# RWKV mixing and a PReLU feed-forward in one kernel: pair 0's v scaling and w^128 on ScalarE, later loads and check, the last sum in two halves

## The chip, the cores and the metric

The kernel runs on one core of a Trainium2 chip. The metric is the device time of one execution in microseconds; the kernel before took 484.07 us (median of three runs). The engines are TensorE (PE, with its weight loads PEld), VectorE (DVE), ScalarE (ACT), GpSimd (POOL) and SyncE (SP), which here only issues DMAs. Each engine works through its own instructions in order and waits on semaphores for the others.

## The reference

A linear recurrence over 768 steps, for 4 batches and 8 heads of 48, and on its output a feed-forward with two weight matrices:

```
state = 0                                     # per batch and head, 48 x 48
for t in range(768):
    cur = outer(u * k[t], v[t])
    y[t] = r[t] @ (state + cur)
    state = w[:, None] * state + outer(k[t], v[t])
x = y as [3072, 384]                          # tokens x (heads * 48)
h = x @ w_in                                  # [3072, 2048]
g = max(h, 0) + alpha * min(h, 0)
out = g @ w_out                               # [3072, 384]
```

## The kernel before

The sequence is cut into six chunks of 128 steps, the heads into four pairs (q = 0 to 3). In a chunk the recurrence becomes products of matrices: with tables of powers of w (`W[q]`, made by `table`) r and k are scaled, their scores are masked and multiplied with v, and a state goes from chunk to chunk. `T[q]` holds the state of a pair. Products of r, u, k give the factors of the diagonal (`diagonal`), one per step, head and batch.

Chunk 0 (`first_chunk`) has no state before it. For each pair: two loads `r`, `k0`, the two products with the table (L447), their product for the factors (L533), the scores on TensorE (L457), the sums that give the factors (L540, into the accumulator `bank`), v times the factors (L464, into `gh`), the mask by VectorE (L477) and by ScalarE with GpSimd (L471, L473), the output (L485, L489), which is split into a high and a low part (L504, L508). `tokens_table` makes `whalf`, the powers of w by token: ScalarE writes scaled rows (L315), TensorE turns them (L322), VectorE copies them (L325); with it the k of chunk 0 are scaled (L431) and the state made (`state`, L521). `w128` holds w^128 (L279). Chunk 1 ("hasty") takes its products from VectorE (L565), transposes k (L303) and writes its diagonal blocks with GpSimd (L594); `burst` does the hand-over from pair to pair (L652, L662).

The feed-forward runs in 96 steps (6 chunks times 16 blocks of 128 hidden units). `m_in` makes a block of h in nine matmuls (L740), ScalarE and VectorE make g and split it into high and low parts (L748 to L753), `m_out` adds it to three accumulators, one for each 128 output columns (k = 0 to 2), in nine matmuls (L774). At the end of a chunk the sums are copied and stored (L801, L803). Weights come as 64-bit numbers and are taken apart by ScalarE and VectorE (`part_of_tile`). `check` tests that the inputs lie in the range that this form needs, and writes a flag; each engine reads it at a set place of the program (L890), and a general loop follows if it is set.

The order of the work is not that of the code: every piece is given an engine, an estimated time, what it reads and writes, and a rank (`add`), and `Plan.in_order` simulates the engines and lets on each the ready piece with the lowest rank go first. `warm` is a matmul on the identity whose result nobody reads; the plan puts such fillers (`fill`) where TensorE would wait before the first `m_out`.

Of the kernel before, what the change touches and what calls it, by code (L numbers as in the profile page):

```python
# [18 lines left out]
L = 128  # L19
C = S // L  # L20
# [47 lines left out]
class Plan:  # L68
# [24 lines left out]
    def in_order(self):  # L93
# [50 lines left out]
        while any(waiting.values()):  # L144
# [34 lines left out]
def rwkv_prelu_kernel(ctx: ExitStack, tc, rk, vkr, wP, uP, u, wall, alpha, w, r_all, k_all, v_all, oT):  # L179
# [93 lines left out]
    def table(m):  # L273
# [5 lines left out]
        add("DVE", 0.1, lambda: nc.vector.tensor_tensor(  # L279
            out=w128()[:, m:m + 1], in0=t()[:, 128:129], in1=t()[:, 128:129], op=ALU.mult), r=[t], w=[(w128, m)],  # L280
            rank=10 * m - 78)

    def negative():
        add("ACT", 0.2, lambda: nc.scalar.activation(minus(), ident2(), AF.Copy, scale=-1.0), r=[ident2], w=[minus],
# [26 lines left out]
    def tokens_table(n, first, at):  # L311
        rows, pt = sb([112, P, L], "g", 3), psum()
        for m in range(P):
            for j in range(n // HI):
                add("ACT", 0.3, lambda m=m, j=j: nc.scalar.activation(  # L315
                    rows()[:, m, HI * j:HI * (j + 1)], W[m]()[:, L - 1:HI - 1:-1], AF.Copy,
                    scale=w128()[:, m:m + 1] if first and j == 0 else W[m]()[:, L:L + 1]),
                    r=[W[m], (w128, m)], w=[(rows, (m, j))], rank=at)
# [5 lines left out]
        add("PE", 0.6, turn, r=[rows, ident], w=[pt], rank=at)  # L324
# [6 lines left out]
    def raw_weights(i, rank, behind=()):  # L331
        t = raws[i] = sb([128, 2 * DM, 2], "wraw", 2, U32)
        for p, cols, by in parts_of(i):
            load((t, p), lambda cols=cols: nc.sync.dma_start(
                t()[:, cols].rearrange("p f a -> p (f a)"), wall[i][:, cols].bitcast(U32)), 768 * by, rank + (p or 0), behind)
        return t

    def parts_of(i):
        return [(p, slice(DM * p, DM * (p + 1)), 0.5) for p in range(2)] if i == 0 else [(None, slice(0, 2 * DM), 1.0)]
# [44 lines left out]
    first_k, first_v = [], []  # L384
# [30 lines left out]
    def inputs(c, q, r, k0, v, k, early):  # L415
        n = 2 * B * D
        moved = [(X[0], (1, 1, 2))] if c == 1 else []
        for j, t in enumerate((r, k0)):
            if c == q == j == 0:
# [7 lines left out]
             early + 0.1 * q + 0.15 if c else -98.85 + 0.1 * q, moved)  # L427
# [9 lines left out]
    def first_chunk(q):  # L437
# [16 lines left out]
        def scores():  # L454
# [5 lines left out]
        add("PE", 1.1, scores, r=[r, k0], w=A, rank=q - 95)  # L460
# [3 lines left out]
        add("DVE", 0.5, lambda: nc.vector.tensor_tensor(  # L464
            out=vc().rearrange("p b (g e) -> p g b e", g=2)[:, :, :, 0:D],
            in0=v().rearrange("p (g b) e -> p g b e", g=2),
            in1=bank()[:, 8 * q:8 * q + 8].rearrange("p (b g) -> p g b", g=2)[:, :, :, None].broadcast_to([128, 2, B, D]),
            op=ALU.mult), r=[(bank, q), v], w=[vc], rank=10 * q - 77)
# [62 lines left out]
    def diagonal(q, r, k0, cu, sums, cols, mine, prod_rank, sum_rank, copy_rank):  # L531
# [11 lines left out]
        add("PE", 0.6, c_sum, r=[prod, uw], w=[mine], rank=sum_rank)  # L543
# [216 lines left out]
    def m_out(n):  # L760
# [10 lines left out]
        def mm(j, ks):  # L771
            a, x = ((wh, gh), (wl, gh), (wh, gl))[j]
            for k in ks:
                nc.tensor.matmul(banks[k](), a[i]()[:, NK + k], x(), start=(begin and j == 0), stop=(end and j == 2))  # L774

        if n == NM - 1:
            for k in range(NK):
                add("PE", 0.7, lambda k=k: [mm(j, (k,)) for j in range(3)], r=[(wh[i], 1), (wl[i], 1), gh, gl], w=[banks[k]],
                    rank=n + MLAG - 0.5)
# [4 lines left out]
        if end:  # L784
            again = c in seen
            seen.add(c)
            for k in range(NK):
# [7 lines left out]
                if again:  # L795
# [3 lines left out]
                        out=o(), in0=t(), in1=o(), op=ALU.add), r=[banks[k]], w=[o], rank=n - 90)  # L799
                else:  # L800
# [7 lines left out]
    def check():  # L808
# [3 lines left out]
        at = 40  # L812
        add("POOL", 0.1, lambda: (ok(), w2(), nc.gpsimd.memset(ok()[:, 0:NF + P], 0.0)), w=[ok], rank=at)
        add("DVE", 0.1, lambda: nc.vector.tensor_scalar(ok()[:, 0:NF], alph(), 1.0, None, op0=ALU.is_le), r=[alph],
            w=[ok], rank=at)
        add("DVE", 0.1, lambda: nc.vector.tensor_tensor(out=w2(), in0=wp(), in1=wp(), op=ALU.mult), r=[wp], w=[w2],
# [42 lines left out]
    jobs.append((40, 7, check))  # L859
# [158 lines left out]
```

## Time and profile before

| what | value |
|---|---|
| median of three runs | 484.07 us (482.76 to 484.35) |
| profiled execution | 483.28 us |
| span of the profile | 481.6 us |
| TensorE busy | 472.8 us, 98% |
| VectorE busy | 312.1 us, 65% |
| ScalarE busy | 244.8 us, 51% |
| GpSimd busy | 97.6 us, 20% |
| granted TensorE clock | 0.999 |

A row of the order in time gives the start, the duration, the engine, the line, the operation, what is written from what is read, and how many instructions are merged in it; in brackets stands the time for which the engine was idle before it, and what ended this. Matmuls are pipelined, so the durations of neighbours overlap.

### The profile page before, as it was taken

What the parts mean: (1) busy time and instruction counts of PE and PEld (TensorE: products, weight loads), DVE (VectorE), ACT (ScalarE), POOL (GpSimd) and SP (SyncE); (2) the same over time, 40 slices, a digit from 0 to 9 for tenths busy, and PEclk for the clock granted to TensorE, in tenths of its full rate; (3) what the DMA queues carried; (4) which work ended last, traced back from release to release, by engine and by line L of the source; (5) the groups of instructions that cost most, each with busy time, mean ns of one, the idle gap of its engine ahead of it and who ended that gap; (6) DMA issues with size and microseconds to landing.
All of it is one profiled execution on the core that took longest, in us unless ns stands there. A gap on an engine that the chain in (4) does not pass through costs nothing. (4 is left out here: it accounts for less than half of the span.)

```text
span 481.6 us, 11276 instructions
## 1 busy us (share of the span) xinstructions
PE 472.8 (98%) x4667; PEld 385.2 (80%) x4667; DVE 312.1 (65%) x519; ACT 244.8 (51%) x554; POOL 97.6 (20%) x119
## 2 busy tenths in 40 slices
PE   8999999999999999999999999999999999999996
PEld 6777777888888888888888888888888878888884
DVE  7999899999787784865755766745634534333331
ACT  3877898766455553553553643544633433433332
POOL 5119890012414021402202301200200000000000
PEclk9999999999999999999999999999999999999999
DMA  7965785632154631531221421200310000100001
GB/s 227 276 231 181 247 248 167 230 125 74 41 174 123 193 116 59 149 91 37 64 78 37 152 86 40 72 26 31 85 37 1 1 1 0 67 0 1 0 1 69
DMA packets 23111, 46.19 MB, mean 96 GB/s; under 512 B 3376, under 2 KB 11184, under 8 KB 23056
## 3 DMA queue, kind: packets, MB, share of 16 engines
q1 hardware_dynamic: 21968, 43.24, 28.4%
q0 software_dynamic: 960, 1.97, 2.0%
q8 instruction: 37, 0.61, 0.5%
q10 hardware_dynamic: 128, 0.23, 0.1%
q14 instruction: 18, 0.15, 0.1%
HBM read 37.17 MB, written 6.29 MB: 90 GB/s over the span
## 5 line engine op out<-in xcount | busy, mean ns | idle before, releaser
L740 PE MATMUL bank<-x,wh 128*128 128x512 f32 x576 | 195.3, 392 | 0.0
L749 DVE SCALAR_TENSOR_TENSOR g<-bank,alph,g 128x512 f32<-128x512 f32 x96 | 71.9, 749 | 104.5 <-ACT g L748 104.2
L740 PEld LDWEIGHTS bank<-x,wh 128*128 128x128 f32 x576 | 108.1, 188 | 23.9 <-issue 0.8
L748 ACT ACTIVATE g<-bank 128x512 f32<-128x512 f32 x96 | 57.2, 596 | 128.2 <-PE bank L740 127.9
L740 PE MATMUL bank<-x,wl 128*128 128x512 f32 x288 | 112.2, 390 | 0.0
L752 ACT ACTIVATE gh<-g 128x512 fp32r<-128x512 f32 x96 | 60.5, 630 | 73.1 <-DVE g L749 73.0
L753 DVE TENSOR_TENSOR gl<-g,gh 128x512 fp32r<-128x512 f32 x96 | 72.0, 750 | 36.7 <-ACT gh L752 35.9
L774 PE MATMUL acc<-gh,wh 128*128 128x512 f32 x288 | 83.2, 396 | 0.0
L774 PE MATMUL acc<-gh,wl 128*128 128x512 f32 x288 | 81.6, 390 | 0.0
L774 PE MATMUL acc<-gl,wh 128*128 128x512 f32 x288 | 81.5, 390 | 0.0
L774 PEld LDWEIGHTS acc<-gh,wl 128*128 128x128 f32 x288 | 53.9, 188 | 11.4
L774 PEld LDWEIGHTS acc<-gl,wh 128*128 128x128 f32 x288 | 53.9, 188 | 11.3
L740 PEld LDWEIGHTS bank<-x,wl 128*128 128x128 f32 x288 | 54.1, 188 | 10.9
L774 PEld LDWEIGHTS acc<-gh,wh 128*128 128x128 f32 x288 | 52.7, 188 | 11.6 <-issue 0.4
L582 POOL TENSOR_TENSOR rr<-rr,kk 128x384 f32<-128x384 f32 x16 | 20.2, 1261 | 164.0 <-DMA kk<-vkr 89.2
L598 ACT ACTIVATE base<-ident,cu 128x64 f32<-128x64 f32 x128 | 32.9, 337 | 1.8 <-DVE cu L588 1.8
L594 POOL TENSOR_SCALAR base<-ident,cu 128x64 f32<-128x64 f32 x32 | 30.7, 983 | 13.7 <-ACT cu L546 13.7
L406 DVE TENSOR_TENSOR x<-bank,x 48x256 fp32r<-48x256 f32 x64 | 27.0, 422 | 1.3
L390 POOL DMA_DIRECT2D x<-x x30 | 15.4, 519 | 60.6 <-ACT o L801 49.4
L568 DVE TENSOR_TENSOR raw<-raw,W 112x512 f32<-112x512 f32 x32 | 23.7, 764 | 2.5 <-DMA raw<-rk 2.5
L405 ACT ACTIVATE x<-bank 48x256 fp32r<-48x256 f32 x64 | 24.2, 378 | 2.1 <-PE bank L662 1.0
L584 POOL TENSOR_TENSOR rr<-rr,utab 128x384 f32<-128x384 f32 x16 | 22.9, 1429 | 1.2
(116 smaller groups left out, 397.6 us busy)
## 6 DMA issues: line engine op xcount, KB each, us to landing
wraw<-wall SPq DMA_DIRECT2D x15, 768.0 KB, 4.6
raw<-rk SPq DMA_DIRECT2D x45, 224.0 KB, 3.7
v<-vkr SPq DMA_DIRECT2D x24, 192.0 KB, 3.6
kk<-vkr SPq DMA_DIRECT2D x20, 192.0 KB, 4.0
rr<-vkr SPq DMA_DIRECT2D x16, 192.0 KB, 2.5
oT<-o SPq DMA_DIRECT2D x12, 256.0 KB, 2.2
x<-x POOLq DMA_DIRECT2D x30, 64.0 KB, 2.6
oT<-g SPq DMA_DIRECT2D x6, 256.0 KB, 3.4
```

The costliest lines, as they stand in the source:

```text
L405: add("ACT", us, lambda: nc.scalar.activation(h(), view(), AF.Copy), r=[src], w=parts(x, 0, ps), rank=rank)
L406: add("DVE", us + 0.1, lambda: nc.vector.tensor_tensor(out=l(), in0=view(), in1=h(), op=ALU.subtract), r=[src] + parts(x, 0, ps), w=parts( ...
L568: add("DVE", 0.72, lambda t=t, tab=tab: nc.vector.tensor_tensor(out=t().rearrange("p b (j t) -> p (b j) t", j=2), in0=t().rearrange("p b ( ...
L584: add("POOL", 1.2, lambda: nc.gpsimd.tensor_tensor(out=rt().rearrange("p (g b) e -> p g b e", g=2), in0=rt().rearrange("p (g b) e -> p g b ...
L594: add("POOL", 1.0, lambda g=g, b=b: nc.gpsimd.tensor_scalar(base()[:, g, b], ident2(), cu()[:, g, b:b + 1], None, op0=ALU.mult), r=[cu, id ...
L598: add("ACT", 0.32, lambda g=g, b=b: nc.scalar.activation(base()[:, g, b], ident2(), AF.Copy, scale=cu()[:, g, b:b + 1]), r=[cu, ident2], w ...
L740: nc.tensor.matmul(hp()[:, :], a[i]()[:, k], X[c]()[:, x, k], start=(k == 0 and j == 0), stop=(k == NK - 1 and j == 2))
L748: add("ACT", 0.6, lambda: nc.scalar.activation(g(), hp()[:, :], AF.Copy), r=[hp], w=[g], rank=n - 100)
L749: add("DVE", 0.75, lambda: nc.vector.scalar_tensor_tensor(out=g(), in0=hp()[:, :], scalar=alph()[:, i:i + 1], in1=g(), op0=ALU.mult, op1=A ...
L752: add("ACT", 0.64, lambda: nc.scalar.activation(gh(), g(), AF.Copy), r=[g], w=[gh], rank=n - 100)
L753: add("DVE", 0.73, lambda: nc.vector.tensor_tensor(out=gl(), in0=g(), in1=gh(), op=ALU.subtract), r=[g, gh], w=[gl], rank=n - 99)
L774: nc.tensor.matmul(banks[k](), a[i]()[:, NK + k], x(), start=(begin and j == 0), stop=(end and j == 2))
```

## The change

Seven things are changed. (1) For pair 0 of chunk 0, v times its factors is done by ScalarE: one instruction copies the factors, eight multiply a 128x48 piece each. (2) w^128 is made by ScalarE, and the rows for whalf of chunk 0 are one instruction per pair instead of two, in another buffer, earlier. (3) v of chunk 0 is loaded later than r and k0 of the next pairs. (4) The check waits for the last weights. (5) The raw weights of blocks 13 to 15 are loaded in halves. (6) Fillers stand behind the sums of pairs 0 and 1, no longer ahead of the scores of pairs 1 to 3; the planner counts small DMAs otherwise. (7) In the last two steps the matmuls go column block by column block, and the last block's sum is made in two halves of 256 tokens, copied by ScalarE and VectorE, stored from SP's and ScalarE's queue.

```diff
-                dma = max(dma, p.end + 1.5) + p.kb / DMA_RATE
-                p.end = dma + 0.3
+                if p.kb < 16:
+                    p.end += 1.7
+                else:
+                    dma = max(dma, p.end + 1.5) + p.kb / DMA_RATE
+                    p.end = dma + 0.3
...
-        add("DVE", 0.1, lambda: nc.vector.tensor_tensor(
-            out=w128()[:, m:m + 1], in0=t()[:, 128:129], in1=t()[:, 128:129], op=ALU.mult), r=[t], w=[(w128, m)],
-            rank=10 * m - 78)
+        add("ACT", 0.2, lambda: nc.scalar.activation(
+            w128()[:, m:m + 1], t()[:, 128:129], AF.Copy, scale=t()[:, 128:129]), r=[t], w=[(w128, m)], rank=-46)
...
-        for p, cols, by in parts_of(i):
+        for p, cols, by in halves if i == 0 or i >= 13 else parts_of(i):
...
-             early + 0.1 * q + 0.15 if c else -98.85 + 0.1 * q, moved)
+             early + 0.1 * q + 0.15 if c else -98.76 + 0.2 * q, moved)
...
+        if q < 1:
+            factors = sb([128, 2, B], "cu", 2)
+            add("ACT", 0.25, lambda: nc.scalar.activation(
+                factors(), bank()[:, 8 * q:8 * q + 8].rearrange("p (b g) -> p g b", g=2), AF.Copy), r=[(bank, q)],
+                w=[factors], rank=q - 93.9)
+            for b in range(B):
+                for g in range(2):
+                    add("ACT", 0.32, lambda b=b, g=g: nc.scalar.activation(
+                        vc()[:, b, HI * g:HI * g + D], v()[:, g * B + b], AF.Copy, scale=factors()[:, g, b:b + 1]),
+                        r=[factors, v], w=[(vc, (b, g))], rank=q - 93.9)
+        else:
...
-        if n == NM - 1:
+        halves = [slice(0, NT // 2), slice(NT // 2, NT)]
+        if n >= NM - 2:
             for k in range(NK):
...
+                        rank=NM + MLAG - 2.5 + (0.1, 0.2, 0.5)[k] + (0.2 + 0.01 * p) * (n == NM - 1))
...
+                elif n == NM - 1 and k == NK - 1:
+                    for p, cols in enumerate(halves):
+                        if p == 0:
+                            add("ACT", 0.38, lambda o=o, t=banks[k], cols=cols: nc.scalar.activation(
+                                o()[:, cols], t()[:, cols], AF.Copy), r=[(banks[k], p)], w=[(o, p)], rank=n - 90)
+                        else:
+                            add("DVE", 0.42, lambda o=o, t=banks[k], cols=cols: nc.vector.tensor_copy(
+                                o()[:, cols], t()[:, cols]), r=[(banks[k], p)], w=[(o, p)], rank=n - 90)
+                        eng, name = ((nc.sync, "SP"), (nc.scalar, "ACT"))[p]
...
-        at = 40
+        at = 24
...
+    for p in first_scores[1:]:
+        fill[p] = 0
```

The order of VectorE from the first table on, before: `W_95` and `W_96` are the tables of pairs 0 and 1, `g` the product for the sums, `gh` the scaled v.

```order
L275 SCALAR_TENSOR_TENSOR W_95<-wp,unit 112x65
L278 RECIPROCAL W_95<-W_95 112x64
L447 TENSOR_TENSOR raw<-raw,W_95 112x512 x2
L533 TENSOR_TENSOR g<-raw 112x512
L275 SCALAR_TENSOR_TENSOR W_96<-wp,unit 112x65
L278 RECIPROCAL W_96<-W_96 112x64
L447 TENSOR_TENSOR raw<-raw,W_96 112x512 x2
L279 TENSOR_TENSOR w_99<-W_95 112x1
L533 TENSOR_TENSOR g<-raw 112x512
L464 TENSOR_TENSOR gh<-v,acc_162 128x2x4x48
L477 COPY_PREDICATED below_135<-strict,bank_142 128x512
```

The same place on VectorE now:

```order
L278 SCALAR_TENSOR_TENSOR W_95<-wp,unit 112x65
L281 RECIPROCAL W_95<-W_95 112x64
L278 SCALAR_TENSOR_TENSOR W_96<-wp,unit 112x65
L450 TENSOR_TENSOR raw<-raw,W_95 112x512
L281 RECIPROCAL W_96<-W_96 112x64
L450 TENSOR_TENSOR raw<-raw,W_95 112x512
L547 TENSOR_TENSOR g<-raw 112x512
L450 TENSOR_TENSOR raw<-raw,W_96 112x512 x2
L547 TENSOR_TENSOR g<-raw 112x512
L491 COPY_PREDICATED below_135<-strict,bank_142 128x512
```

The table of pair 1 has moved ahead of and in between pair 0's products, and w^128 and the scaled v are gone.

VectorE again, from the mask of pair 2 to the products of pair (1,0) now (before, the copy of whalf and the four scalings of kk stood behind L565, the products of raw with `W_95` for chunk 1):

```order
L491 COPY_PREDICATED below_135<-strict,bank_145 128x512
L326 COPY whalf<-bank_142 128x384
L368 SCALAR_TENSOR_TENSOR wx<-wx,low 128x384
L377 SCALAR_TENSOR_TENSOR wx<-wraw,wx 128x384
L491 COPY_PREDICATED gl<-strict,acc_409 128x512
L478 TENSOR_TENSOR gh<-v,acc_162 128x2x4x48
L381 TENSOR_TENSOR wl_118<-wx,wh_102 128x384
L434 TENSOR_TENSOR kk<-kk,whalf 128x384
L368 SCALAR_TENSOR_TENSOR wx<-wx,low 128x384
L434 TENSOR_TENSOR kk<-kk,whalf 128x384 x2
L377 SCALAR_TENSOR_TENSOR wx<-wraw,wx 128x384
L434 TENSOR_TENSOR kk<-kk,whalf 128x384
```

L582, the products for chunk 1, follows two rows below these.

ScalarE behind the rows of `pick`, now; before, `minus` and the two copies of scores followed there at once:

```order
L282 ACTIVATE w_99<-W_95 112x1
L316 ACTIVATE base<-W_95,w_99 112x128
L282 ACTIVATE w_99<-W_96 112x1
L316 ACTIVATE base<-W_96,w_99 112x128
L485 ACTIVATE below_136<-bank_143 128x512
L469 ACTIVATE cu<-acc_162 128x8
L474 ACTIVATE gh<-v,cu 128x48 x8
L485 ACTIVATE gl<-acc_280 128x512
```

Between the copies of pair 0's and pair 1's scores stand the factors and the eight products.

The end of TensorE, before: `acc_4969`, `acc_4971`, `acc_4973` are the sums of k = 0, 1, 2.

```order
L774 MATMUL acc_4969<-gh,wh_117 128x512
L774 MATMUL acc_4969<-gh,wl_133 128x512
L774 MATMUL acc_4969<-gl,wh_117 128x512
L774 MATMUL acc_4971<-gh,wh_117 128x512
L774 MATMUL acc_4971<-gh,wl_133 128x512
L774 MATMUL acc_4971<-gl,wh_117 128x512
L774 MATMUL acc_4973<-gh,wh_117 128x512
L774 MATMUL acc_4973<-gh,wl_133 128x512
L774 MATMUL acc_4973<-gl,wh_117 128x512
```

And now, with `acc_4970` as k = 2:

```order
L791 MATMUL acc_4968<-gh,wh_117 128x512
L791 MATMUL acc_4968<-gh,wl_133 128x512
L791 MATMUL acc_4968<-gl,wh_117 128x512
L791 MATMUL acc_4970<-gh,wh_116 128x512
L791 MATMUL acc_4970<-gh,wl_132 128x512
L791 MATMUL acc_4970<-gl,wh_116 128x512
L791 MATMUL acc_4970<-gh,wh_117 128x256
L791 MATMUL acc_4970<-gh,wl_133 128x256
L791 MATMUL acc_4970<-gl,wh_117 128x256
L791 MATMUL acc_4970<-gh,wh_117 128x256
L791 MATMUL acc_4970<-gh,wl_133 128x256
L791 MATMUL acc_4970<-gl,wh_117 128x256
```

The sums of k = 0 and 1 are complete nine matmuls ahead of the end, and k = 2 comes last in two halves.

## Rows read from the trace of the kernel before

**Rows 1.** Stretches: us, busy PE, PEld, DVE, ACT, POOL, clock, DMA share, GB/s.

```profile
5.00:10.00 5.00, 4.93 (x62) 3.78 (x60) 4.69 (x9) 0.85 (x2) 2.51 (x6) 1.00 0.95 268
25.00:43.00 18.00, 17.50 (x225) 13.72 (x223) 17.76 (x31) 13.77 (x26) 8.82 (x8) 1.00 0.57 183
90.00:470.00 380.00, 380.00 (x3506) 313.99 (x3505) 228.66 (x378) 174.50 (x404) 51.29 (x54) 1.00 0.22 67
```

**Rows 2.** Order in time, VectorE, from the first table to the check.

```profile
4.28 1.35 DVE L447 TENSOR_TENSOR raw<-raw,W 112x512 f32<-112x512 f32 x2
...
6.27 0.29 DVE L275 TENSOR_TENSOR_SCAN W<-wp,unit 112x65 f32<-112x65 f32 x1
...
7.18 0.69 DVE L447 TENSOR_TENSOR raw<-raw,W 112x512 f32<-112x512 f32 x1
8.08 0.69 DVE L447 TENSOR_TENSOR raw<-raw,W 112x512 f32<-112x512 f32 x1 [0.21 <-DMA raw<-rk]
...
9.80 0.54 DVE L464 TENSOR_TENSOR gh<-v,acc 128x384 f32<-128x384 f32 x1
...
22.21 0.17 DVE L814 TENSOR_SCALAR ok<-alph 128x16 f32<-128x16 f32 x1
...
22.76 0.55 DVE L378 TENSOR_TENSOR wl<-wx,wh 128x384 fp32r<-128x384 f32 x1
...
25.77 0.55 DVE L325 COPY whalf<-bank 128x384 f32<-128x384 f32 x1
...
28.24 0.95 DVE L374 SCALAR_TENSOR_TENSOR wx<-wraw,wx 128x768 uint32<-128x768 uint32 x1
...
31.78 0.68 DVE L533 TENSOR_TENSOR g<-raw 112x512 f32<-112x512 f32 x1
```

**Rows 3.** Groups of instructions to 92 us: busy, mean ns, idle before.

```profile
L652 PE MATMUL bank<-raw,T 48*48 48x64 f32 x128 | 3.0, 221 | 1.0 <-ACT x L717 0.7 <-DVE base L681 0.3
...
L279 DVE TENSOR_TENSOR w<-W 112x1 f32<-112x1 f32 x4 | 1.0, 259 | 0.0
...
L322 PE MATMUL bank<-ident,g 112*128 112x112 f32 x4 | 0.5, 258 | 0.0
```

**Rows 4.** Order in time, TensorE, at the start and the fillers.

```profile
6.28 1.16 PE L457 MATMUL bank<-raw 48*128 48x128 f32 x16
7.37 0.63 PE L540 MATMUL acc<-uw,g 112*64 112x2 f32 x16
7.94 0.83 PE L834 MATMUL acc<-ident 128*128 128x256 bf16 x6
...
25.36 0.39 PE L834 MATMUL acc<-ident 128*128 128x256 bf16 x2
25.91 0.60 PE L303 MATMUL bank<-ident,raw 112*128 112x112 f32 x4 [0.16 <-DVE raw L565]
...
30.91 0.82 PE L834 MATMUL acc<-ident 128*128 128x256 bf16 x6
```

**Rows 5.** Order in time, ScalarE, two scaled rows of 112x64.

```profile
17.51 0.37 ACT L315 ACTIVATE g<-W,w 112x64 f32<-112x64 f32 x1
17.75 0.37 ACT L315 ACTIVATE g<-W 112x64 f32<-112x64 f32 x1
```

**Rows 6.** The tail: order in time, the last store's landing, its stretch.

```profile
476.23 0.39 PE L774 MATMUL acc<-gh,wl 128*128 128x512 f32 x1
...
476.45 0.39 PE L774 MATMUL acc<-gl,wh 128*128 128x512 f32 x1
476.94 0.60 ACT L801 ACTIVATE g<-acc 128x512 f32<-128x512 f32 x1
477.56 0.33 SPq L803 DMA_DIRECT2D oT<-g  x1
...
oT<-g SPq DMA_DIRECT2D x1, 256.0 KB, 2.2
...
477.00:479.00 2.00, 0.00 (x0) 0.00 (x0) 0.00 (x0) 0.54 (x1) 0.00 (x0) 1.00 0.99 375
```

More of the change, by code (lines that the diff above doesn't have):

```diff
@@ L311, in tokens_table @@
     def tokens_table(n, first, at):
-        rows, pt = sb([112, P, L], "g", 3), psum()
+        rows, pt = sb([112, P, L], "base" if first else "g", 3), psum()
         for m in range(P):
[L314 to L318, printed above, removed]
+            add("ACT", 0.3 + 0.1 * first, lambda m=m: nc.scalar.activation(
+                rows()[:, m, 0:n], W[m]()[:, L - 1::-1] if first else W[m]()[:, L - 1:HI - 1:-1], AF.Copy,
+                scale=w128()[:, m:m + 1] if first else W[m]()[:, L:L + 1]),
+                r=[W[m], (w128, m)], w=[(rows, m)], rank=at)
         def turn():
@@ L336, in raw_weights @@
         return t
+    halves = [(p, slice(DM * p, DM * (p + 1)), 0.5) for p in range(2)]
     def parts_of(i):
-        return [(p, slice(DM * p, DM * (p + 1)), 0.5) for p in range(2)] if i == 0 else [(None, slice(0, 2 * DM), 1.0)]
+        return halves if i == 0 else [(None, slice(0, 2 * DM), 1.0)]
     def weights(i, need):
@@ L541, in c_sum @@
                                      stop=True, skip_group_check=True)
-        add("PE", 0.6, c_sum, r=[prod, uw], w=[mine], rank=sum_rank)
+            if cu is None:
+                for _ in range((3, 2, 0, 0)[q]):
+                    warm()
+        add("PE", 0.6 + (0.13 * (3, 2, 0, 0)[q] if cu is None else 0), c_sum, r=[prod, uw], w=[mine], rank=sum_rank)
         if cu is None:
@@ L769, in m_out, with mm @@
         acc_of.append(acc[2])
-        def mm(j, ks):
+        def mm(j, ks, cols=slice(0, NT)):
             a, x = ((wh, gh), (wl, gh), (wh, gl))[j]
             for k in ks:
-                nc.tensor.matmul(banks[k](), a[i]()[:, NK + k], x(), start=(begin and j == 0), stop=(end and j == 2))
-        if n == NM - 1:
+                nc.tensor.matmul(banks[k]()[:, cols], a[i]()[:, NK + k], x()[:, cols], start=(begin and j == 0),
+                                 stop=(end and j == 2), skip_group_check=c == C - 1 and k == NK - 1)
+        halves = [slice(0, NT // 2), slice(NT // 2, NT)]
+        if n >= NM - 2:
             for k in range(NK):
-                add("PE", 0.7, lambda k=k: [mm(j, (k,)) for j in range(3)], r=[(wh[i], 1), (wl[i], 1), gh, gl], w=[banks[k]],
-                    rank=n + MLAG - 0.5)
+                for p, cols in enumerate(halves if n == NM - 1 and k == NK - 1 else [slice(0, NT)]):
+                    add("PE", 0.7 if n < NM - 1 or k < NK - 1 else 0.35,
+                        lambda k=k, cols=cols: [mm(j, (k,), cols) for j in range(3)],
+                        r=[(wh[i], 1), (wl[i], 1), gh, gl], w=[banks[k] if n < NM - 1 or k < NK - 1 else (banks[k], p)],
+                        rank=NM + MLAG - 2.5 + (0.1, 0.2, 0.5)[k] + (0.2 + 0.01 * p) * (n == NM - 1))
         else:
```

28 lines of the change are left out of this document (16 added, 12 removed).

## The prediction

> **What bounds the kernel now.** I read the busy time by stretch first [rows 1]. From 90 to 470 us TensorE is busy 380.00 of 380.00 us: the matmuls of the second half of the kernel stand one behind the other, their number does not change, and no edit in that stretch can shorten the time. Time can come only from before, where TensorE waits or runs fillers, and from the tail behind the last matmul. In the first 43 us the full engine is VectorE: 4.69 of 5 us at 5 to 10, 17.76 of 18 at 25 to 43, while ScalarE has 0.85 of 5 at 5 to 10.
>
> The second view is the order in time on VectorE [rows 2]. The reader is to see a chain without holes: tables, products, the scaling of v, weight pieces, with one wait of 0.21 us at 8.08 for a load. Third, TensorE in order of time [rows 4]: its own waits look small because fillers were put where the planner expected a hole. Six fillers stand at 7.94 (0.83 us), two at 25.36 with a wait behind them until the transposes at 25.91 (0.55), six at 30.91 (0.82). Further on, the hand-over matmuls of L652 (four bursts in chunk 1) wait 1.0 us [rows 3]. So TensorE loses 3.2 us that a quicker VectorE could give back. Last the tail [rows 6]: the last matmul starts at 476.45 and takes 0.39, ScalarE copies for 0.60 from 476.94, the store is issued at 477.56 and lands 2.2 us later, at 479.76; the span ends 1.84 us after that.
>
> The profiled execution took 483.28 us, 1.68 outside its span of 481.6; the median of the three runs is 484.07 (482.76 to 484.35). The sum is made against 483.28, and the gain is then taken from the median.
>
> **The change part by part.**
>
> *What VectorE loses.* The four w^128 instructions go, 1.0 us together [rows 3]; one product of v and its factors goes, 0.54; the first four instructions of the check go from here, 0.55 from 22.21 to the next at 22.76; and the wait of 0.21 goes, because pair 1's two loads now stand ahead of v's in SP's queue [rows 2]. That is 2.30. Neighbours on this engine overlap a little (the pair at 4.28 lasts 1.35 for two), for which I take off 0.3: 2.0 us. Nothing new stands on VectorE, so the product that starts at 31.78 should start at about 29.8. The last three of the check leave too, later.
>
> *What VectorE does in another order.* Table 1 (scan and reciprocal, 0.91 us from 6.27 to 7.18) now stands between pair 0's products, which end at 4.28 + 1.35 + 0.91 = 6.54 and not at 5.63. TensorE's scores began at 6.28, behind the fillers, so they begin 0.3 us later. The copy of whalf and the four k scalings (25.77 to 28.24, 2.47 us) now stand ahead of pair (1,0)'s products, which were ready at 25.77: 25.77 - 2.0 + 2.47 = 26.2. The transposes that wait for them (25.91 before) start at 26.3. In exchange two of the four state products, and whalf's transposes, are already done on TensorE by then, and the fillers at 25.36 and 30.91 are gone.
>
> *What TensorE can give back.* Of 0.83 + 0.55 + 0.82 = 2.2 us of fillers, 0.3 is lost at the first scores: 1.9. Both counts, 2.0 by VectorE and 1.9 by TensorE, meet near the same size; I take the smaller. Bounds: nothing, if a new wait stands where a filler stood, and 1.9 + 1.0 = 2.9 if the waits of L652 go as well.
>
> *What ScalarE takes.* Eight instructions of 128x48 with a scale per partition. The nearest rows are those of 112x64 with such a scale: 0.37 us each, 0.24 from start to start (17.51 to 17.75) [rows 5]. That makes 8 x 0.24 = 1.9 us, at most 8 x 0.37 = 3.0 and, since a shorter tile can be quicker, perhaps 1.6. They begin when the factors are there: scores from 6.58, sums 1.09 later as now (6.28 to 7.37), 0.63 for the sums [rows 4], so 8.3, and with the copy of the factors about 8.5. They end at 10.4 (10.1 to 11.5). ScalarE's hole there covers it: 4.15 of 5 us are free at 5 to 10 [rows 1]. In the worst case pair 0's output on TensorE comes a microsecond later than with 10.4, which the wait until 26.3 behind it takes up. w^128 and the table rows are short and fall into the same hole; ScalarE's evacuations of pair 1 queue behind the eight, and VectorE is not behind those.
>
> The Trainium skill, "ScalarE: Activation LUTs", section "Rules for kernel authors", says to use VectorE and not ScalarE for copies and multiplications. By that rule this part loses: one instruction of 0.54 us becomes eight of 1.9. The trace decides for the edit as long as the hole stands, since it is the full engine that gets lighter.
>
> *Loads and flag.* Bytes stay the same; three weight loads become six, each a further issue of 0.33 us (the issue at 477.56 [rows 6]), for weights that TensorE needs in a stretch without a wait. SP now reads the flag later in its queue, ahead of loads for chunk 3, and would hold these back if the check were late; the check's input is done long before. Both at nothing; without that cover 3 x 0.33 = 1.0 us.
>
> *The tail.* Columns k = 0 and 1 are finished two groups earlier, so their stores are out of the way. At present all three stores run together: the DMA engines are 0.99 busy from 477 to 479 [rows 6]. The last half is copied by VectorE (half of ScalarE's 0.60, with a fixed part: 0.3 to 0.5, I take 0.42), and its store carries 128 KB: 2.2 us less half of what 256 KB take at 375 GB/s (0.34), so 1.86, or up to 2.2 if the fixed part is all of it; I take 2.0. It lands 0.1 + 0.42 + 0.02 + 2.0 = 2.54 us after the last matmul, now 479.76 - 476.84 = 2.92: 0.38 gained. Against it stand six matmuls of 256 columns for three of 512. No row shows one. At half the time each they cost nothing, at the full 0.22 (476.23 to 476.45) 0.66. The nearest rows are four transposes of 112 columns with a full weight load in 0.55 us [rows 3], about 0.10 from start to start, so a weight load does not hold a matmul above 0.11: I take 0.03. Tail: 0.35 gained, between -0.3 and +0.6.
>
> The Trainium skill's start page, "Trainium Kernel Development and Optimization", section "Key Constraints", says that stores from SP's and ScalarE's queues run on the same 16 DMA engines and that a second queue only saves issue time. The share of 0.99 fits it. By the rule the second queue is worth one issue of 0.33 us at most, and less if the first half's issue is already over; my 0.38 counts nothing for parallel transfers.
>
> Sum: 1.9 + 0.35 = 2.25 us; 483.28 becomes 481.0, and the median 484.07 becomes 481.8.
>
> **The rivals.**
> - *The gain is given back in chunk 1.* TensorE arrives 1.9 us earlier at the bursts of L652, whose bases GpSimd writes and whose states pass through ScalarE, and waits there. For it: those are the only real waits now [rows 3]. Against it: the first link of that chain comes earlier too, as it hangs on the product at 31.78. With 1.5 us given back 0.75 is left: 483.3.
> - *More than forecast.* The waits of 1.0 in L652 vanish with the lead of VectorE: 2.25 + 1.0, 480.8. The second half of the check leaving VectorE speaks for it.
> - *Slower.* ScalarE's queue is served in order, and the new order puts weight pieces, which wait for VectorE, ahead of the copies of y out of PSUM that TensorE's next step needs. The wait of 0.7 us on ScalarE in L652 [rows 3] is of this kind. If each of the four bursts waits 1.0 more, that is 4.0 - 2.25 = 1.75 lost: 485.8. It decides once each wait grows by more than 2.25/4 = 0.56. ScalarE's light load in the beginning speaks against it.
> - *The change doesn't do what it says.* TensorE's clock is granted at 1.00, the 2.4 GHz level, in each stretch [rows 1], with fillers right ahead of pair 0's and pair 1's scores; some of these are gone or moved. If the clock were at 1.2 GHz for the scores and sums up to 10 us, some 2 us of work, they would take 2 us more and the gain at the start were gone: only the tail is left, 483.7.
>
> The Trainium skill, "TensorE: Matmul & The Clock Gate", section "Why this matters for your kernels", warns that idle gaps between bursts of matmuls send the clock back to half rate. By that rule the place to look at is the hole ahead of 26.3, about 1 us by my count, where fillers stood; no row of before shows a fall during the work, so it gives no price.
>
> **How the numbers follow.** Forecast 481.8 with a chance of 0.52; more 0.13; given back 0.22; clock 0.04; slower 0.09. Its own range is 480.5 to 483. The range for 8 in 10 runs from 479.8, both bounds of the gains together (2.9 + 0.6 = 3.5) and the spread of the runs, to 484.2, which takes in the rival of the given-back gain. A difference of 0.3%, 1.45 us, is about what a measurement of this kernel can tell from no change: below 482.6 is faster. Nearly all of the first two cases lie there, 0.65 together; the two next are no change, 0.26; slower 0.09.
>
> **What would show it.** In the changed profile: VectorE's product for the sums of pair (1,0) starts near 29.8; the eight ScalarE instructions start near 8.5 and end before 11, before the output of pair 0 on TensorE; TensorE's first transposes of chunk 1 start near 26.3, without fillers ahead; the last matmul near 475 and the last store's landing 2.5 us behind it. The forecast is wrong if L652 waits more than 2 us in all, if the scores of pair 0 start later than 7, if the halved matmuls stand more than 0.15 us apart, or if the granted clock is under 1.00 anywhere between 6 and 470 us.

## The result, and the profile of the changed kernel

The changed kernel is slower by about half a per cent, where the prediction said faster. With two more runs the median of the kernel before is 483.21 us, no longer 484.07. A ratio, here and below, is worked out from all runs of both kernels and is not the quotient of the two medians.

| | before | changed |
|---|---|---|
| median, runs | 483.21 us, 5 (482.75 to 484.35) | 485.65 us, 5 (485.26 to 486.38) |
| ratio | | 1.0055 [1.0042, 1.0067] |
| profiled execution, its span | 483.28, 481.56 | 486.38, 484.66 |
| TensorE idle, 90 to 470 us | 0.00 us | 2.16 us |
| last matmul's end to the span's end | 4.72 us | 5.62 us |

The spans differ by 3.1 us: 2.2 have been lost when the last matmul ends (479.04 against 476.84), 0.9 come behind it. The profiled execution of the changed kernel is the slowest of its five, so the account below covers 3.1 us, while the medians differ by 2.4. The stretches of [rows 1] now read as follows, with the one added in which all the idle time lies:

```profile
5.00:10.00 5.00, 4.01 (x68) 3.17 (x66) 4.56 (x7) 3.02 (x12) 2.92 (x7) 1.00 1.03 270
25.00:43.00 18.00, 17.97 (x220) 13.80 (x220) 16.80 (x27) 14.28 (x28) 9.31 (x12) 1.00 0.66 220
90.00:470.00 380.00, 377.84 (x3494) 311.64 (x3493) 227.40 (x382) 173.36 (x402) 49.69 (x54) 1.00 0.22 66
...
129.00:134.00 5.00, 2.84 (x130) 2.37 (x130) 3.03 (x5) 2.59 (x6) 1.83 (x2) 1.00 0.29 88
```

**The start gained, but half of the forecast.** ScalarE's eight instructions take 1.91 us from 8.44, as forecast. VectorE's product of pair (1,0) starts at 30.62, 1.16 earlier than in [rows 2], where 2.0 were forecast. TensorE gets a new wait of 1.37 us, for a copy of x by ScalarE. In order of time on the three engines:

```profile
8.44 1.91 ACT L474 ACTIVATE gh<-v,cu 128x48 f32<-128x48 f32 x8
...
22.14 0.51 PE L522 MATMUL bank<-x,less 128*128 128x512 f32 x1 [1.37 <-ACT x L518]
...
30.62 0.68 DVE L547 TENSOR_TENSOR g<-raw 112x512 f32<-112x512 f32 x1
```

TensorE reaches the first burst of chunk 2 (the matmuls of L669, L652 before) at 129.10 instead of 130.04: 0.94 us gained, where 1.9 were forecast.

**At 129 us this is lost, three times over.** VectorE in order of time, changed kernel:

```profile
124.90 0.55 DVE L605 TENSOR_REDUCE cu<-rr 128x8 f32<-128x384 f32 x1
125.37 0.74 DVE L766 SCALAR_TENSOR_TENSOR g<-bank,alph,g 128x512 f32<-128x512 f32 x1
126.81 0.69 DVE L770 TENSOR_TENSOR gl<-g,gh 128x512 fp32r<-128x512 f32 x1 [0.70 <-ACT gh L769]
129.49 0.56 DVE L434 TENSOR_TENSOR kk<-kk,whalf 128x384 f32<-128x384 f32 x1 [1.99 <-POOL rr L599]
129.97 0.75 DVE L766 SCALAR_TENSOR_TENSOR g<-bank,alph,g 128x512 f32<-128x512 f32 x1
```

and the same place in the kernel before, with TensorE's burst and ScalarE's small copy L675 (L692 now):

```profile
127.80 0.74 DVE L749 SCALAR_TENSOR_TENSOR g<-bank,alph,g 128x512 f32<-128x512 f32 x1
129.42 0.56 DVE L431 TENSOR_TENSOR kk<-kk,whalf 128x384 f32<-128x384 f32 x1 [0.87 <-POOL rr L582]
...
130.04 0.67 PE L652 MATMUL bank<-raw,T 48*48 48x64 f32 x32
131.03 0.14 ACT L675 ACTIVATE seen_y<-bank 1x2 f32<-1x2 f32 x1
```

The planner has put two instructions in the other order. The scaling of k of pair (3, 0) overwrites what GpSimd's product over rr still reads, so it waits; the product with the slopes of step 19 (L766, L749 before) waits for nothing, but now stands behind it. It reads a PSUM bank that TensorE's burst wants. ScalarE's work on step 19 comes 2.2 us late as well, and with it the small copy L692 for which the rest of the burst waits. TensorE and ScalarE, in order of time:

```profile
129.10 0.32 PE L669 MATMUL bank<-raw,T 48*48 48x64 f32 x4
130.77 0.59 PE L669 MATMUL bank<-raw,T 48*48 48x64 f32 x26 [1.35 <-DVE g L766]
...
133.19 0.14 ACT L692 ACTIVATE seen_y<-bank 1x2 f32<-1x2 f32 x1
133.39 0.32 PE L679 MATMUL bank<-base,v 64*48 64x64 f32 x7 [0.81 <-ACT seen_y L692]
```

From this burst to the next it is 17.13 us now (129.10 to 146.23) and was 14.44 (130.04 to 144.48): 2.69 lost.

**A small one at 152 us.** The check's two matmuls, at 24.9 us in the kernel before, now stand in the full stretch:

```profile
152.19 0.39 PE L757 MATMUL bank<-x,wh 128*128 128x512 f32 x1
152.51 0.21 PE L858 MATMUL bank<-ok,one 128*1 128x20 f32 x2
152.65 0.96 PE L791 MATMUL acc<-gh,wh 128*128 128x512 f32 x3
153.45 0.40 PE L791 MATMUL acc<-gh,wl 128*128 128x512 f32 x1
```

From 152.19 to 153.45 there are 1.26 us for four large matmuls that take 4 x 0.227 elsewhere: 0.35 more. From the next burst to the one behind it (146.23 to 163.07, before 144.48 to 160.96) it is 16.84 us instead of 16.48.

**The tail** [rows 6], last matmuls, copies, stores, and the stores' landing:

```profile
478.76 0.28 PE L791 MATMUL acc<-gl,wh 128*128 128x256 f32 x1
479.14 0.38 ACT L825 ACTIVATE g<-acc 128x256 f32<-128x256 f32 x1 [0.85 <-PEq L931]
479.55 0.33 SPq L831 DMA_DIRECT2D oT<-g  x1
479.56 0.42 DVE L828 COPY g<-acc 128x256 f32<-128x256 f32 x1 [3.79 <-ACT g L825]
480.01 0.39 ACTq L831 DMA_DIRECT2D oT<-g  x1
...
oT<-g SPq DMA_DIRECT2D x1, 128.0 KB, 1.7
oT<-g ACTq DMA_DIRECT2D x1, 128.0 KB, 2.6
```

The halves don't run side by side. ScalarE's copy of the first half starts 0.10 after the last matmul of the second, VectorE's copy 0.04 after ScalarE's has ended, so the last store is issued 0.97 behind the last matmul (0.72 before), and it lands after 2.6 us, with half the bytes. The three other profiles with halves (e1, e2, e6) have the copy at 0.10 and the issue at 0.97, too.

The landing is late in one part only. Sixteen updates of a semaphore tell that a store has landed: fifteen stand 1.85 us behind the issue, the last one 0.74 later (0.08 later in the kernel before). The DMA records show where the late share was: its packets begin at 481.76, where a fetch of 8 KB of instructions ends that had begun at 481.00, and the others are through by 481.4. In the kernel before such a fetch begins at 479.06, when the last packets of the store are already running. In e1, e2, e3 and e6 the late share, too, begins within 0.02 us of the end of such a fetch. That the fetch holds it up is read from these records; no run tests it.

Account: -0.94 at the start, +2.69 at the burst, +0.36 for the check's matmuls, +0.90 for the tail (0.60 up to the last landing, 0.29 behind it), together +3.0 of 3.1.

### The profile page after: what moved, and what is told of

Same layout as the page of the kernel before. It is cut to its first block, busy times and chain, and to the rows that moved or that the text cites. A ratio compares the mean times of both kernels' runs of the same rounds, so it can differ in the third digit from the quotient of the medians.

```text
span 484.7 us, 11264 instructions
## 1 busy us (share of the span) xinstructions
PE 471.9 (97%) x4659; PEld 384.1 (79%) x4659; DVE 311.3 (64%) x515; ACT 247.8 (51%) x563; POOL 91.2 (19%) x119
## 5 line engine op out<-in xcount | busy, mean ns | idle before, releaser
L766 DVE SCALAR_TENSOR_TENSOR g<-bank,alph,g 128x512 f32<-128x512 f32 x96 | 71.9, 749 | 105.0 <-ACT g L765 103.4
L791 PE MATMUL acc<-gh,wh 128*128 128x512 f32 x289 | 84.2, 397 | 0.0
L599 POOL TENSOR_TENSOR rr<-rr,kk 128x384 f32<-128x384 f32 x16 | 18.5, 1156 | 168.1 <-DMA kk<-vkr 91.8
L611 POOL TENSOR_SCALAR base<-ident,cu 128x64 f32<-128x64 f32 x32 | 26.5, 850 | 17.3 <-ACT cu L563 17.3
L585 DVE TENSOR_TENSOR raw<-raw,W 112x512 f32<-112x512 f32 x32 | 22.3, 724 | 3.1 <-DMA raw<-rk 3.1
L601 POOL TENSOR_TENSOR rr<-rr,utab 128x384 f32<-128x384 f32 x16 | 21.7, 1356 | 1.2
```

The lines of the kernel that those rows point to most:

```text
L585: add("DVE", 0.72, lambda t=t, tab=tab: nc.vector.tensor_tensor(out=t().rearrange("p b (j t) -> p (b j) t", j=2), in0=t().rearrange("p b ( ...
L601: add("POOL", 1.2, lambda: nc.gpsimd.tensor_tensor(out=rt().rearrange("p (g b) e -> p g b e", g=2), in0=rt().rearrange("p (g b) e -> p g b ...
L611: add("POOL", 1.0, lambda g=g, b=b: nc.gpsimd.tensor_scalar(base()[:, g, b], ident2(), cu()[:, g, b:b + 1], None, op0=ALU.mult), r=[cu, id ...
L766: add("DVE", 0.75, lambda: nc.vector.scalar_tensor_tensor(out=g(), in0=hp()[:, :], scalar=alph()[:, i:i + 1], in1=g(), op0=ALU.mult, op1=A ...
L791: nc.tensor.matmul(banks[k]()[:, cols], a[i]()[:, NK + k], x()[:, cols], start=(begin and j == 0), stop=(end and j == 2), skip_group_check ...
```

## Experiments

Ratios are to the kernel before on the same chip; 0.001 is 0.48 us. The intervals are 0.8 to 1.7 us wide, so a difference of a few tenths between two runs is read from the profiles, if at all. "Piece" is what the planner orders.

| run | median us | before us | ratio, 95% interval |
|---|---|---|---|
| e1_swap | 483.95 | 483.04 | 1.0012 [1.0002, 1.0022] |
| e2_check_behind | 486.48 | 483.04 | 1.0072 [1.0056, 1.0088] |
| e3_tail_whole | 485.34 | 483.04 | 1.0051 [1.0033, 1.0069] |
| e4_before_swap | 484.99 | 483.04 | 1.0037 [1.0023, 1.0052] |
| e5_swap_tail | 483.06 | 483.32 | 0.9997 [0.9989, 1.0006] |
| e6_order_only | 485.91 | 483.32 | 1.0051 [1.0036, 1.0067] |
| e7_copies_first | 483.23 | 483.32 | 0.9998 [0.9985, 1.0011] |
| e8_v_vector | 483.10 | 483.32 | 1.0000 [0.9985, 1.0014] |
| e9_v_vector | 482.50 | 482.67 | 0.9999 [0.9987, 1.0011] |
| e10_before_v | 482.90 | 482.67 | 1.0001 [0.9990, 1.0012] |
| e11_weights_whole | 482.24 | 482.67 | 0.9986 [0.9977, 0.9995] |
| e12_best | 482.60 | 482.88 | 0.9987 [0.9975, 0.9998] |

### The order on VectorE: e1 and e4

After planning, one piece is moved (e4: the scaling ahead of the product, in the kernel before).

```diff
     order = plan.in_order()
+    order.remove(leaky[19])                              # product of step 19
+    order.insert(order.index(scaled[4]), leaky[19])      # scaling of k, pair (3, 0)
```

> The changed kernel with one exchange on VectorE: the product with the slopes of step 19 stands ahead of the scaling of k of pair (3, 0), which stood ahead of it; nothing else moves. Theory 1 (order): in the changed kernel that scaling waits 1.99 us for GpSimd, the product of step 19 starts at 129.97 for that reason, and TensorE, whose burst wants the PSUM bank that the product reads, stands 1.35 us, and 0.81 us again when ScalarE, pushed back by the same product, frees the other bank late. Then both waits go, step 19's product starts near 128 and the time falls by 2.0 to 2.6, to 483.0 to 483.6. Theory 2 (supply): the burst waits for the scaled k itself, whatever the order, since rr of that pair lands at 128.4; then a wait of 0.8 to 1.3 stands at L643 (L646 in this kernel) in place of the first one, the second goes, and the time is 484.3 to 484.9. Theory 3 (the loss is not in this burst but spread over 90 to 470 us): 485.4 to 485.9.

> The kernel before, with the opposite exchange: the scaling of k of pair (3, 0) ahead of the product with the slopes of step 19, at 127.8 us; nothing else moves. Theory 1 (order): the product starts near 130.0 instead of 127.80, the burst that began at 130.04 waits 0.6 to 0.8 for its bank, the part behind ScalarE's small copy comes 1.8 later, and the time is 484.7 to 485.2. Theory 2 (supply or spread): no wait of TensorE there, 483.0 to 483.5.

e1, VectorE and TensorE in order of time:

```profile
126.68 0.74 DVE L766 SCALAR_TENSOR_TENSOR g<-bank,alph,g 128x512 f32<-128x512 f32 x1
128.65 0.56 DVE L434 TENSOR_TENSOR kk<-kk,whalf 128x384 f32<-128x384 f32 x1 [1.23 <-POOL rr L599]
...
128.56 0.66 PE L669 MATMUL bank<-raw,T 48*48 48x64 f32 x32
129.05 0.41 PE L679 MATMUL bank<-base,v 64*48 64x64 f32 x16
129.27 0.57 PE L643 MATMUL bank<-v,kk 64*64 64x48 f32 x30
```

e4, the kernel before with the opposite exchange, VectorE and TensorE:

```profile
129.86 0.56 DVE L431 TENSOR_TENSOR kk<-kk,whalf 128x384 f32<-128x384 f32 x1 [1.57 <-POOL rr L582]
130.34 0.74 DVE L749 SCALAR_TENSOR_TENSOR g<-bank,alph,g 128x512 f32<-128x512 f32 x1
...
131.14 0.59 PE L652 MATMUL bank<-raw,T 48*48 48x64 f32 x26 [0.40 <-DVE g L749]
133.76 0.44 PE L662 MATMUL bank<-base,v 64*48 64x64 f32 x16 [0.82 <-ACT seen_y L675]
```

Order it is, from both sides. In e1 the scaling still waits, TensorE does not: from burst to burst 14.44 us, as before, TensorE is busy 380.00 of 380.00, and the ratio falls by 0.0043, 2.1 us, where its profile gives back 2.69. In e4 the stretch grows by 1.78 and the time by 0.0037, 1.8 us. The theory of supply falls: though GpSimd's product ends the scaling's wait in each of these runs, the burst wants the scaled k late enough.

### The check ahead of the sum: e2

```diff
+    for p in checks:                  # its four VectorE pieces, collected as they are added
+        order.remove(p)
+    at = order.index(sums_of[3]) + 1  # behind the sum that frees rr
+    order[at:at] = checks
```

> The changed kernel with the check's four small VectorE instructions (0.54 us from 124.36 on) put behind the sum over rr that they stood ahead of; nothing else moves. That sum frees the single rr buffer for the next load. If the chain sum, load of rr, GpSimd's two products, scaling of k sets when the burst at 129 us goes on, everything from the load on comes 0.5 earlier, the scaling of k starts near 129.0 instead of 129.49, and the time falls by 0.4 to 0.6, to 485.1 to 485.25. If the load's landing is set by something else (the queue, GpSimd), the scaling stays at 129.4 to 129.5 and the time within 0.15 of 485.65.

SyncE, GpSimd and VectorE in order of time:

```profile
123.61 0.54 DVE L605 TENSOR_REDUCE cu<-rr 128x8 f32<-128x384 f32 x1
...
124.18 0.33 SPq L597 DMA_DIRECT2D rr<-vkr  x1
...
127.64 1.01 POOL L599 TENSOR_TENSOR rr<-rr,kk 128x384 f32<-128x384 f32 x1 [5.83 <-DMA rr<-vkr]
128.68 0.56 DVE L434 TENSOR_TENSOR kk<-kk,whalf 128x384 f32<-128x384 f32 x1 [1.93 <-POOL rr L599]
```

The second theory holds, by the distance to the burst. The scaling starts 0.8 us earlier than in the changed kernel, but there TensorE's burst is 0.54 later as well. In e1, whose burst starts at the same time (128.56 in both), the load is issued at 124.74, and here at 124.18; GpSimd starts at 127.60 and 127.64. Landing took 3.3 us instead of 2.7. Again one share of sixteen is late: fifteen updates stand at 126.57 (127.06 in e1), the last at 127.48 (127.44). A 16 KB fetch of instructions runs from 125.07 to 126.19 here, and the late packets begin at 126.19; in e1 it runs from 125.09 to 126.02. The landing fits the end of the fetch better than the issue, but no run moves the fetch. The time did not fall: 486.48 is above both forecasts, and the interval reaches that of the changed kernel.

### The tail: e3, e5 and e6

e3 makes the last block whole again, e6 takes back the order of the last two steps, e5 both, with e1's exchange.

```diff
-        if n >= NM - 2:                         # e5, e6: if n == NM - 1
...
-                for p, cols in enumerate(halves if n == NM - 1 and k == NK - 1 else [slice(0, NT)]):
+                for p, cols in enumerate([slice(0, NT)]):        # e3, e5
```

> The changed kernel with the last 512 columns in one piece again: three matmuls of 512 columns, one copy by ScalarE, one store of 256 KB from SyncE's queue; the rest, the order of the last two steps among it, stays. Theory 1 (the halves run one behind the other): from the end of the last matmul to the end of the span 4.76 as before instead of 5.66, time 484.6 to 484.9. Theory 2 (the prediction's: halves gain 0.35): time 485.9 to 486.1. Theory 3 (the tail is as long either way): 485.5 to 485.8.

> The changed kernel with the exchange on VectorE of e1, and with the whole end as in the kernel before: step 94's output matmuls matrix by matrix again, only step 95's block by block, and the last block in one piece. Theory 1 (order of the end): the changed kernel sums blocks 0 and 1 earlier against the last matmul, so their stores start 1.4 and 0.7 us ahead of it instead of 0.7 and 0, while a 16 KB fetch of instructions is running; the second store's issue took 0.97 and 0.82 us in two such ends instead of 0.33, and the last store waits behind. With the old end the stretch from the last matmul to the end of the span is 4.5 to 4.8 instead of 5.6 to 5.7, every issue 0.33, and the time 0.8 to 1.0 below that of e1 (483.95), 482.9 to 483.2. Theory 2 (something else of the changed kernel, such as where the flag is read, makes the end longer): 5.5 to 5.7 again and 483.7 to 484.1.

> The changed kernel with step 94's output matmuls matrix by matrix and step 95's block by block, as in the kernel before, but with the last block in two halves, copied and stored as in the changed kernel. Theory 1 (order): from the last matmul to the end of the span 4.8 to 5.1, being 4.76 and 0.25 for the two copies one behind the other at most; time 485.0 to 485.3 against 485.65. Theory 2 (the halves cost by themselves, by the second queue's store that lands after 2.6): 5.5 to 5.7, time 485.5 to 485.8. Theory 3 (the prediction's gain of halves shows once the order is old): 4.3 to 4.5.

From the last matmul's end, in us:

| | to the last landing | from there to the end | semaphore waits of SyncE in it |
|---|---|---|---|
| before: old order, whole | 2.96 | 1.77 | 2 |
| e5: old order, whole | 2.91 | 2.15 | 7 |
| e6: old order, halves | 3.59 | 2.06 | 6 |
| e3: new order, whole | 3.45 | 2.15 | 7 |
| changed: new order, halves | 3.56 | 2.06 | 6 |

Either edit alone makes the landing 0.5 to 0.7 later; both cost no more than one. So e3 and e6 hardly gain (1.0051 each, against 1.0055), and e5 gains 0.7 over e1. Its tail of 5.06 lies between its two theories; the landing is as before, and the rest are the waits. My first theory for e3, the halves alone, was wrong, and so was that for e6, the order alone. With the new order the issue of the second store is held up; e3, in order of time:

```profile
476.80 1.65 SPq L838 DMA_DIRECT2D oT<-o  x2
...
478.28 0.60 ACT L836 ACTIVATE g<-acc 128x512 f32<-128x512 f32 x1 [0.82 <-PEq L931]
478.90 0.33 SPq L838 DMA_DIRECT2D oT<-g  x1
...
oT<-g SPq DMA_DIRECT2D x1, 256.0 KB, 2.7
```

Two issues last 1.65 in all, with 0.97 for the second (1.01 and 0.33 in e11 below), and the last store lands after 2.7 instead of 2.2. It is issued 0.72 behind the last matmul, as before, and fifteen of its updates stand after 2.0 us (2.2 before); only the last is 0.74 later. The DMA records have a 16 KB fetch of instructions from 476.73 to 478.07 there, and from 475.37 to 476.32 in the kernel before, ahead of its second store at 476.82. That this fetch is what holds the second issue is not shown.

### The start: e7 to e10

e7 is e5 with a copy of x on ScalarE moved ahead of two weight pieces. e8 and e9 take v's product back to VectorE, with the old end; in e8 step 19's product stood behind its readers, so that e8 leaves the slopes out of this step. e10 is the kernel before with that one edit.

```diff
+    order = [p for p in order[:upto + 1] if p not in held] + held + order[upto + 1:]   # e7
...
-        if q < 1:                     # e8, e9: if False (v times its factors on VectorE)
```

> e5 with one more exchange, on ScalarE: the copy of x of pair 1 (L518 at 21.49 in the changed kernel) ahead of two instructions on the weights, one of which waits 1.45 us for VectorE; one piece on VectorE (the low part of those weights) moves behind a scaling of k with it. TensorE's wait of 1.2 to 1.4 us for that copy goes in every theory. Theory 1 (VectorE sets the first 43 us, as the prediction read it): the time given back is lost again before step 8, whose product starts within 0.3 us of e5's, and the times are equal within 0.3. Theory 2 (TensorE or ScalarE sets it): step 12's product starts 0.8 to 1.2 earlier than in e5 and the time is 0.8 to 1.2 below it.

> e5 with pair 0's v times its factors on VectorE in one instruction, as in the kernel before, instead of ScalarE's nine; the planner orders the rest anew. Theory 1 (that move gives most of what the changed kernel wins in the first 100 us): step 12's product starts 1.0 to 1.9 later than in e5, and the time is 0.8 to 1.9 above it. Theory 2 (the win comes from the other edits of the start, the loads, the planner's price of small loads, the fillers): within 0.4 of e5 at step 12 and in time.

> e8 once more, without the exchange of step 19's product, which in e8 put that product behind the instructions that read it (step 19 was summed from values without the slopes there) and which the planner's order of this kernel does not need: pair 0's v times its factors on VectorE in one instruction, the end as in the kernel before, all else as changed. Theory 1 (that move to ScalarE gives most of the win of the first 100 us): step 12's product 0.8 to 1.9 later than in e5 and e7, time 483.9 to 484.9. Theory 2 (the other edits of the start give it, as e8's 483.1 hints): the burst at 129 us starts within 0.6 of e5's, time 482.7 to 483.4.

> The kernel before with one edit alone: pair 0's v times its factors by ScalarE, a copy of the factors and eight 128x48 instructions. Theory 1 (it takes 0.47 us of VectorE's work in the first 10 us away, and VectorE sets the first 43 us): the burst at 130 us starts 0.4 to 1.0 earlier than in the kernel before and the time is 482.2 to 482.9. Theory 2 (pair 0's sums are not late on VectorE but on the loads, so it gives nothing alone): 483.0 to 483.7; and if ScalarE's 1.9 us put the copies behind them late, 483.7 to 484.5.

e7, TensorE and ScalarE in order of time:

```profile
20.28 0.50 PE L522 MATMUL bank<-x,less 128*128 128x512 f32 x1
...
24.04 0.50 PE L522 MATMUL bank<-x,less 128*128 128x512 f32 x1 [1.35 <-ACT x L518]
...
22.09 0.92 ACT L365 ACTIVATE low<-wraw 128x768 uint32<-128x768 uint8 x1 [1.22 <-DVE wx L368]
```

The wait of 1.34 ahead of pair 1's L522 in e5 is gone, and 1.35 stand ahead of pair 2's: the next weight piece on ScalarE waits for VectorE instead. Times are equal (0.9998 and 0.9997), which fits the reading that VectorE sets this stretch. That the wait goes "in every theory" was wrong.

e8 and e9 equal e5 in time, within intervals of 0.6 to 0.7 us to either side, and e9's burst starts at 128.46 (e5 129.17): the start has its gain without the move of v to ScalarE. Which of the other edits of the start gives it is not tested. e10 is undecided. Its profile has the burst at 128.38, 1.66 earlier, its ratio is 1.0001: the planner orders all that follows anew, and part is lost again (0.3 at the bursts, a tail of 5.18).

One profile shows another loss at the start. e6 differs from the changed kernel only in its end, but its profiled execution, the slowest of seven, ran with TensorE's clock at half early on. Two stretches, with the columns of [rows 1], and TensorE in order of time at either clock:

```profile
8.00:10.00 2.00, 1.01 (x15) 0.72 (x13) 1.54 (x2) 1.12 (x6) 0.64 (x1) 0.99 1.06 308
10.00:16.00 6.00, 6.00 (x54) 4.86 (x54) 5.83 (x12) 2.60 (x11) 0.87 (x1) 0.50 1.05 344
...
13.87 1.95 PE L503 MATMUL bank<-below,v 128*48 128x128 f32 x16
18.88 1.08 PE L503 MATMUL bank<-gl,v 128*48 128x128 f32 x16
```

TensorE waits 0.98 us for a product of VectorE, until 9.48 (that product waited 0.91 for its load), and from 9.94 to 16.77 the granted clock is 0.50, the level of 1.2 GHz. The product of pair (1,0) then starts at 32.53 and the burst of chunk 2 at 131.00, where the seven other profiles with this start have 128.76 in the mean: 2.2 us later. The mean clock of that execution is 0.991. It is under 0.995 in 5 of the 120 runs with the changed start or a part of it (0.990 in one of e2's six), and in none of the 97 on record with the start before. Only e6's was profiled, so what happened in the others is not known; nor is it shown that the wait made the clock fall, since the 1.37 us at L522 in the changed kernel's profile came without a fall.

### The loads and the semaphores: e11 and e12

```diff
-        for p, cols, by in halves if i == 0 or i >= 13 else parts_of(i):
+        for p, cols, by in parts_of(i):
```

> The changed kernel with the end as in the kernel before, and the last three weight tiles loaded whole again; the planner then sets step 19's product ahead of the scaling by itself, without an exchange. Three loads fewer move the last store back to the seventh of the eight DMA semaphores that SyncE waits for one after the other at the end (0.07 to 0.09 us each); in e5 it had the second and six waits stood behind it. Theory 1: from the last matmul to the end 4.7 to 4.8 instead of 5.04, time 0.2 to 0.4 below e5's 483.06. Theory 2 (the order of the semaphores is nothing): 5.0 to 5.3 and 483.0 to 483.3. Theory 3 (whole loads of 768 KB hold up the loads of chunk 2 and TensorE waits between 90 and 130 us): over 483.4.

> e9 and e11 together: the changed kernel with the end as in the kernel before, the last three weight tiles loaded whole, and pair 0's v times its factors on VectorE. Theory 1 (each loss found is separate): TensorE waits nowhere between 90 and 470 us, the burst at 129 us starts 1.2 to 1.6 earlier than in the kernel before, the check's two small matmuls still cost 0.36 near 150, the end takes 4.6 to 4.8, and the time is 0.4 to 0.8 below the kernel before of the same chip, with its interval below 1. Theory 2 (the start of e9 was a lucky execution, or whole loads undo it): within 0.3 of the kernel before.

e11, the tail in order of time:

```profile
475.27 1.01 SPq L838 DMA_DIRECT2D oT<-o  x2
...
476.06 0.60 ACT L836 ACTIVATE g<-acc 128x512 f32<-128x512 f32 x1
476.68 0.33 SPq L838 DMA_DIRECT2D oT<-g  x1
```

The span ends at 480.6, 4.67 behind the last matmul, with two semaphore waits and 1.77 behind the landing, as in the kernel before. Here the planner has step 19's product first without help, and TensorE waits nowhere from 90 to 470 us. The ratio is 0.0011 below e5's, 0.5 us, of which 0.38 is seen in the tail; e5's profile also takes 0.52 longer from the second burst of chunk 2 to the third (17.36 us, 16.84 in e11). e11 and e12 are the two versions below the kernel before; they keep the new start and leave the tail, the split loads and (e12) v's move out. e11 has the tail of the kernel before, no wait in the full stretch and the check's 0.36, and is 0.0014 faster, 0.7 us: so the start is worth about 1 us, with 0.4 to either side, if these parts add up. e12's burst starts at 130.14 in its profile, 1.68 later than in e9, which differs only in the weight loads: so the second theory's lucky start is part of the truth. With v on ScalarE the burst starts between 128.46 and 129.17 in the seven profiles at full clock, against 130.04 and 130.42 in two of the order before.

## Why the prediction was wrong

**The step that failed** is the one on which the sum was built: "no edit in that stretch can shorten the time". I read TensorE's 380.00 of 380.00 us [rows 1] as a stretch to leave out of the sum, and priced only what could be won. With the same matmuls a full stretch can't be shortened, but it can be lengthened, and the edits shift the planner's order far behind the place that they name. In that stretch the changed kernel loses 2.69 us at one burst and 0.36 at the check's matmuls. e1 gives the first back, by one exchange.

- *VectorE's chain, 2.0 us earlier.* Right in direction, and in size only in some executions: the product starts at 30.62 here and at 29.75 to 30.33 in e1, e2, e3, e5, e7 and e11, forecast 29.8. In e6, at half the clock, it was 32.53. The transposes of chunk 1 came at 27.21, in e1 at 26.34; forecast 26.3.
- *TensorE gives back 1.9.* Too much. At the burst of chunk 2 it is 0.94 in the profile and 1.5 in the mean of the seven profiles at full clock (128.76 against 130.23). The fillers are gone, but waits came in their place, which the prediction had only as its lower bound: 1.37 at L522, behind ScalarE's copy of x. The scores started at 5.99, 0.3 earlier than before and not 0.3 later.
- *ScalarE's eight.* Right in every number (8.44, 1.91, 10.35), but no use is seen: e9 is as fast without them. The Trainium skill, "ScalarE: Activation LUTs", section "Rules for kernel authors", says to multiply on VectorE and not on ScalarE; these runs show no loss from the move either (e8, e9 and e10 stand within 0.0003 of their partners, with intervals of 0.0011 to 0.0015 to either side).
- *Loads and flag at nothing.* Wrong twice. The end of the program was not looked at: three more loads move the last store from the seventh to the second of eight semaphores, or with the halves to the third: 0.38 or 0.29. The check was priced for its reads alone; its two matmuls cost 0.36.
- *Tail, 0.35 gained.* Wrong in sign: 0.90 lost, 0.29 of it the loads' semaphores just named. I had the halves overlap, and the landing of 2.54 us behind the last matmul is 3.56. The size of the transfer was right, since fifteen shares of the last store land after 1.85 us (2.0 taken); the copy was 0.4 later than taken, and the sixteenth share 0.74 behind the others. The 256-column matmuls did keep pace, 0.12 apart. The Trainium skill ("Trainium Kernel Development and Optimization", section "Key Constraints") says that a second queue saves issue time only; here it saved none, since SyncE's issue was over at 479.88 and ScalarE's began at 480.01. No run compares the two queues.
- *The rivals.* The slower one came near in number, 485.8 against 485.65 us, by luck. It had the mechanism, a piece that waits standing in an engine's queue ahead of one that frees PSUM, and the wrong place: ScalarE in chunk 1. There a wait of 1.4 us did come (L522 behind the copy of x), and e7 shows that nothing is won by moving the copy ahead there. In the changed kernel's profile none of the four signs of being wrong came: the bursts of chunk 1 wait 0.1 us in all, the scores started before 7, the halved matmuls stand 0.12 apart, and the clock is 1.00 in each stretch of work. All four looked where the loss was not. The rival of the clock, at 0.04, did come in another execution of the same start (e6), behind a wait of TensorE and with about the price given, 2.2 us against 2; it has no part in the 3.1.

## What to carry to other kernels

An engine that is full with the same work before and after says that nothing can be won in a stretch, not that nothing can be lost there: where a planner or scheduler decides the order, compare the orders of the helper engines far downstream too, and look for an instruction that waits placed ahead of one that frees a PSUM bank. Price small instructions by the stretch in which they land, since two matmuls of 20 columns cost 0.36 us where TensorE has no hole. Before a last tile is halved, look whether the first half can start ahead of the second; here the copy of the first half came behind the matmuls of the whole, and the second copy behind the first.

## What the runs showed that I had not expected

- At the end SyncE passes the eight semaphores that the transfers use in turn, one after the other, 0.07 to 0.09 us each. From the last landing to the end it is 1.77, 2.06 or 2.15 us with 2, 6 or 7 of these waits left, the same to 0.01 in all runs; three loads fewer (e11) bring back the 1.77.
- A load of 192 KB issued 0.56 us earlier landed at the same time (e2). Here and in the late stores of the tail one share of sixteen is late, and its packets begin where a fetch of instructions ends. That the fetch is the cause is not tested.
- Profiles of nearly the same start differ at the first burst of chunk 2 by 1.7 us at full clock (e9 and e12), and by 2.2 us where the clock was at half for 6.8 us (e6), so a gain of 1 us at the start is not to be read from one profile.
